# Four bit-operation steps moved in VectorE's queue, and 33 matmuls of nothing in the first three pairs of heads

## The chip, the cores and the metric

The kernel runs on one core of one Trainium2 chip. The metric is the device time of one execution in microseconds (us), the smaller the better. TensorE is PE in the rows, and its weight loads are PEld; VectorE is DVE, ScalarE is ACT, GpSimd is POOL, and SyncE, whose queue issues nearly all DMAs here, is SP.

## The reference, cut to what matters

Three layers follow one another: causal attention with a decay, a gated dense layer, and a layer of eight experts in which each token goes to one.

```python
# attention: q, k, v are (4, 8, 576, 64), f is (4, 8, 576)
scores = q @ k.T / 8 + (cum[:, None] - cum[None, :])   # cum = cumsum(log f)
attn   = softmax(where(causal, -1e9, scores))
x      = attn @ v                                      # -> (2304, 512)
# dense layer
a, b = x @ w1, x @ w2                                  # 512 -> 1024
x    = ((a * b) @ w3) @ w_out                          # the kernel uses Wc = w3 @ w_out
# experts, 8 of them, the one of the largest gate logit
out[mask] = gate * eom * (relu(x[mask] @ w1[e]) @ w2[e])
```

## The kernel before, in words

**Pairs of heads.** Attention works on 16 pairs of heads, n = 0 to 15. Each pair goes through named stages: loads (lk, lq, lv), the rounded high parts of k and q on ScalarE (kh, qh), the scores of the four query blocks and of the last 64 queries on TensorE (X1, X3, X2, X0 and XL, tiles x and xl), their row maxima on VectorE (m1, m3, m2, m0 and mL, line 234), the remainders of k and q on VectorE (kl, ql, line 201), the turn of the maxima (Tm on TensorE, line 241, tc on ScalarE, line 244), their spread by two DMAs into the rows MR (mv, line 174), the transposed scores in four PSUM groups (GA to GD, line 208, from the high parts and the remainders; HA to HD add the decay and the maxima from CK and MR to the same groups), the exponentials (eA to eD, line 270), the causal masks and column sums on GpSimd (a0 to a4, s1 to s3, lines 276 and 288), and the product with v and its sums (p0, p1, p3, su, lines 297 and 313, tile v). ScalarE copies them out (xa, line 317; sa, line 320), SP stores the sums (zs, line 324), and after each fourth pair the sums of a batch are loaded back, inverted on VectorE and stored (rl, rv, rs, lines 333 to 338).

**The order.** Every engine runs its queue strictly in the order of the program. `START` gives each stage a time within its pair, pairs are 9.8 apart (`PERIOD`), and line 378 sorts all stages of all pairs by START + 9.8 n; `AFTER` puts further steps into the last pair's time in the same way. The times only set an order. Those around the change, in the last pair's time, are: mL 3.54, Tm 3.61, tc 3.98, ql 4.35, lv of pair 14 at 5.71, mv 6.59, GA 8.35, HA 8.43, and later xa of pair 14 at 18.04, s1 18.31, rv of pair 11 at 18.4, sa of pair 14 at 18.44, a2 18.51.

**Wc's pieces.** Between the stages the weights w3 and w_out arrive in pieces of 512 KB of 64-bit floats, in the order of line 407 (piece 12 is w_out's j=4, wo4 in the rows; 13 is w04, 14 is w14, 15 is wo5, 16 is w05). `upto(step, n)` (line 460) brings the first n pieces through a step: step 0 is the load on SP (line 439), 1 a copy on ScalarE (446), 2, 3 and 4 are three bit operations on VectorE (448, 450, 452), 5 a rounding on ScalarE, 6 a subtraction on GpSimd. `K4_13` is upto(4, 13), the three bit operations of piece 12; `K0_16` is the load of piece 15. The raw tiles have three buffers, so that the load of piece 15 waits for the last bit operation of piece 12, and the load of piece 16 for that of piece 13. SP issues in order, and what stands behind such a load waits too.

**PSUM.** The scores rotate through three buffers of two banks (`pss`, line 92); the tile v has the remaining two banks, with one buffer (`psv`, line 86). So p0 of a pair writes v only after sa of the pair before has read it. At the start twenty matmuls of a zero tile, 128x512 in bf16, run on TensorE (`warm_up`, line 154).

Of the kernel before, what the change touches and what calls it, by code (L numbers as in the profile page):

```python
# [11 lines left out]
F32 = mybir.dt.float32  # L12
# [3 lines left out]
BF16 = mybir.dt.bfloat16  # L16
# [12 lines left out]
P = 128  # L29
# [29 lines left out]
}  # L59
SHIFT = {}  # L60

AFTER = {
    "K4_13": 3.595, "K0_15": 3.605, "K0_16": 3.615, "K4_14": 3.625, "K0_17": 3.635, "inputs": 11.329, "scores": 13.382,
    "K1_15": 18.064, "K1_16": 18.074, "K4_15": 18.084, "K0_18": 18.094, "K4_16": 18.104, "P0": 28.286, "P1": 28.296,
    "P2": 28.306, "P3": 28.316,
}


# [6 lines left out]
def attention(nc, tc, ident, xT, rz, xs, wc, q, k, v, f):  # L75
# [6 lines left out]
    V, A, G, PE, SP = nc.vector, nc.scalar, nc.gpsimd, nc.tensor, nc.sync  # L82
    with (
# [6 lines left out]
        inputs, scores = ExitStack(), ExitStack()  # L90
# [10 lines left out]
        def decay_parts():  # L101
            SP.dma_start(out=fc, in_=f)
            V.tensor_scalar(out=fc, in0=fc, scalar1=1e-4, scalar2=1.0, op0=ALU.max, op1=ALU.min)
            A.activation(out=fc, in_=fc, func=ACTF.Ln)
            V.tensor_tensor_scan(c8, fc, fc, 0.0, ALU.add, ALU.bypass)
            V.tensor_scalar(out=EK[0:NH], in0=c8, scalar1=-8.0, scalar2=None, op0=ALU.mult)
            V.scalar_tensor_tensor(out=EK[NH:], in0=c8, scalar=-8.0, in1=EK[0:NH].bitcast(F32), op0=ALU.mult, op1=ALU.subtract)
# [15 lines left out]
        def rows(e, t):  # L123
            e.memset(t.bitcast(F32), 0.0)
            for h in range(2):
                e.memset(t[64 * h:64 * h + 3, :min(S, t.shape[1])].bitcast(F32), 1.0)

        def constants():
            rows(G, CKs[0])
            rows(V, OQ)  # L130
            for t in (OD, *QDs, *[t[:, S:] for x in KHs for t in x]):
                V.memset(t.bitcast(F32), 0.0)
            for h in range(2):
                V.memset(OD[64 * h:64 * h + 3, HALF[h]].bitcast(F32), 1.0)
                for t in (OQ, OD):
                    V.memset(t[64 * h:64 * h + 1].bitcast(F32), 0.0)
            V.memset(ones, 1.0)
            for t in Ms:
                V.memset(t, 0.0)
            G.memset(tri, 0.0)  # L140
            G.affine_select(
                out=tri[:, 512:640], in_=tri[:, 512:640], pattern=[[-1, P]],
                compare_op=ALU.is_ge, fill=NEG, base=0, channel_multiplier=1,
            )
            G.memset(tril, 0.0)
            for h in range(2):
                G.affine_select(
                    out=tril[64 * h:64 * h + 64, 512:S], in_=tril[64 * h:64 * h + 64, 512:S],
                    pattern=[[-1, SL]], compare_op=ALU.is_ge, fill=NEG, base=0, channel_multiplier=1,
                )  # L150
            for t in MRs + CKs[1:]:
                rows(G, t)

        def warm_up():

            z = p1.tile([P, 512], BF16, name="warm")
            V.memset(z, 0.0)
            ps = pss.tile([P, 1024], F32, name="warm", tag="s")
            for _ in range(WARM):
                PE.matmul(ps[:, 0:512], z[:, :P], z, start=True, stop=True)  # L160

        st = {}
# [215 lines left out]
        order = [(START[x] + SHIFT.get((n, x), 0.0) + PERIOD * n, n, i, x) for n in range(B * NP) for i, x in enumerate(START)]  # L378
        order = sorted(order + [(t + PERIOD * (B * NP - 1), B * NP, 0, x) for x, t in AFTER.items()])
        with tc.manual_schedule():  # L380
            warm_up()
            decay_parts()
            constants()
            for _, n, _, x in order:
                if x == "inputs":
                    inputs.close()
                    continue
                if x == "scores":
                    scores.close()
                    wc.banks(0)  # L390
                    continue
                if n == B * NP:
                    if x[0] == "K":
                        wc.upto(int(x[1]), int(x[3:]))
                    else:
                        wc.product(*wc.steps.pop(0))
                    continue
                fn, *args = stages[x]
                fn(st[n], *args)


class Combined:
# [801 lines left out]
def program(shapes):  # L1204
    nc = bacc.Bacc("TRN2", target_bir_lowering=False, num_devices=1)
    a = {n: nc.dram_tensor(n, s, mybir.dt.from_np(t), kind="ExternalInput").ap() for n, (s, t) in shapes.items()}
    out = nc.dram_tensor("out", (N, DM), F32, kind="ExternalOutput").ap()
    with tile.TileContext(nc) as tc:
        with tc.tile_pool(name="keep", bufs=1) as keep, tc.tile_pool(name="raws", bufs=2, reuse_waits="tile") as raws, tc.tile_pool(name="div", bufs=1, space=DRAM) as div:
            rz = div.tile([NP, 2, N], F32, name="rz")  # L1210

            xs = div.tile([E * N, DM + 2], F32, name="xs")
            ident = keep.tile([P, P], F32, name="ident")
            make_identity(nc, ident)
            xpool = ExitStack()
            xt = xpool.enter_context(tc.tile_pool(name="xt", bufs=1, side="right"))
            xT = xt.tile([P, NP, N], F32, name="xT")
            region = ExitStack()
            region.enter_context(tc.manual_schedule())
            wc = Combined(nc, tc, xpool, raws, a["wo"], a["w3t"])  # L1220
            attention(nc, tc, ident, xT, rz, xs, wc, a["q"], a["k"], a["v"], a["f"])
            moe(nc, tc, ident, xT, rz, xs, xpool, raws, region, wc, a["w1"], a["w2"], a["gates"], a["e1"], a["e2"], out)
            xpool.close()
    return nc
# [9 lines left out]
```

## Time and profile before

| | |
|---|---|
| median of 3 runs | 854.89 us (850.76 to 856.73) |
| the profiled execution | 857.55 us, span 855.9 us |
| mean granted clock of TensorE | 0.971 of full speed |
| TensorE busy | 800.8 us (94%), 5140 matmuls |
| VectorE, ScalarE, GpSimd busy | 453.7 us, 280.7 us, 373.6 us |

All times in rows are us from the start of the span. The attention part takes about the first 213 us; after it come the products of Wc, the dense layer and the experts. In a row of the order of time, the bracket at the end is the time that the engine stood idle before the row and what ended that. A clock of 1.00 is full speed (2.4 GHz), 0.50 the half (1.2 GHz).

### The profile page before, as it was taken

The numbers are of one execution on the slowest core, as the hardware profiler recorded it, in microseconds if no ns is written. First come the engines' busy times: TensorE is split into PE (matmuls) and PEld (weight loads), VectorE is DVE, ScalarE is ACT, GpSimd is POOL, SyncE is SP. The second block draws the span as 40 slices with busy tenths as digits, with TensorE's granted clock in tenths as the row PEclk, the third lists the DMA queues.
The fourth block names the chain that finished last, engine by engine and source line by source line (L and its number), as shares of the span: only waits on it lengthen the run. The fifth ranks groups of instructions, "written<-read, shape, count | busy, mean of one in ns | idle before, by whom it ended". The sixth has DMA issues, their size and how long they took to land.

```text
span 855.9 us, 13772 instructions
## 1 busy us (share of the span) xinstructions
PE 800.8 (94%) x5140; PEld 654.6 (76%) x5140; DVE 453.7 (53%) x950; ACT 280.7 (33%) x536; POOL 373.6 (44%) x383
## 2 busy tenths in 40 slices
PE   6899989977999899999999999998799999999995
PEld 4666666655887577888788788897588899999983
DVE  7588888872698860341333223135456846346430
ACT  3466655642454422221221221222122222232321
POOL 5578887883574570131013021023245543354521
PEclk7799999996999999999999999999999999999998
DMA  3446666522445211100010010033556654566460
GB/s 113 135 134 198 216 216 211 157 78 84 129 169 171 87 42 35 50 23 28 25 38 19 7 50 1 1 123 124 173 148 221 201 202 138 183 204 209 149 256 28
DMA packets 40340, 102.12 MB, mean 119 GB/s; under 512 B 8610, under 2 KB 9314, under 8 KB 40016
## 3 DMA queue, kind: packets, MB, share of 16 engines
q1 hardware_dynamic: 37088, 91.46, 33.7%
q0 software_dynamic: 3184, 9.77, 3.0%
q8 instruction: 41, 0.67, 0.3%
q14 instruction: 27, 0.22, 0.1%
HBM read 84.47 MB, written 16.51 MB: 118 GB/s over the span
## 4 chain that ended last, share of the span: by engine, by line
PE 63%; DVE 16%; DMA 9%; issue 7%; ACT 2%; SPq 1%; POOL 0%; POOLq 0%; DVEq 0%; ACTq 0%
DVE junk L234 5%; PE y L541 4%; PE y L539 4%; PE y L540 4%; PE h L541 3%; PE h L539 3%; PE h L540 3%; DMA xs<-xr,pos 3%; PE a L539 3%; PE b L539 3%; PE a L541 3%; PE a L540 3%; PE b L540 3%; PE b L541 3%; PE q L539 2%
## 5 line engine op out<-in xcount | busy, mean ns | idle before, releaser
L569 DVE TENSOR_TENSOR ga<-b,ga 128x512 f32<-128x512 f32 (+1 forms) x40 | 25.4, 635 | 149.6 <-PE b L541 146.5
L684 POOL DMA_INDIRECT xs<-xr,pos x18 | 18.9, 1050 | 187.9 <-DVE pos L680 130.6
L234 DVE CUSTOM_DVE_ANT_0 junk<-x,tri 128x256 f32<-128x256 f32 (+3 forms) x128 | 62.7, 489 | 10.4 <-PE x L208 1.3
L539 PE MATMUL h<-gh,ah 128*128 128x320 f32 (+4 forms) x224 | 67.2, 300 | 0.0
L540 PE MATMUL h<-gl,ah 128*128 128x320 f32 (+4 forms) x224 | 66.9, 299 | 0.0
L541 PE MATMUL h<-gh,al 128*128 128x320 f32 (+4 forms) x224 | 66.9, 299 | 0.0
L276 POOL TENSOR_SCALAR_AFFINE_SELECT PT<-PT 128x256 f32<-128x256 f32 (+1 forms) x80 | 42.6, 545 | 48.5 <-ACT PT L270 48.1
L541 PE MATMUL a<-xh,w1l 128*128 128x512 f32 (+1 forms) x160 | 59.8, 374 | 3.0 <-POOL w1l L457 3.0
L539 PE MATMUL a<-xh,w1h 128*128 128x512 f32 (+1 forms) x160 | 60.8, 380 | 1.9 <-ACT w1h L455 1.9
L539 PE MATMUL b<-xh,w2h 128*128 128x512 f32 (+1 forms) x160 | 60.5, 378 | 0.0
L539 PE MATMUL y<-raw,gh 128*128 128x512 f32 x144 | 58.4, 406 | 1.6 <-ACT gh L570 1.6
L540 PE MATMUL b<-xl,w2h 128*128 128x512 f32 (+1 forms) x160 | 60.0, 375 | 0.0
L540 PE MATMUL a<-xl,w1h 128*128 128x512 f32 (+1 forms) x160 | 59.9, 374 | 0.0
L541 PE MATMUL b<-xh,w2l 128*128 128x512 f32 (+1 forms) x160 | 59.3, 371 | 0.0
L541 PE MATMUL y<-raw,gl 128*128 128x512 f32 x144 | 57.4, 398 | 0.9 <-DVE gl L572 0.9
L540 PE MATMUL y<-raw,gh 128*128 128x512 f32 x144 | 57.6, 400 | 0.0
L532 POOL TENSOR_SCALAR bh<-rb 128x1024 fp32r<-128x1024 f32 x28 | 36.0, 1284 | 47.8 <-DMA rb<-e 41.6
L570 ACT ACTIVATE gh<-ga 128x512 fp32r<-128x512 f32 (+1 forms) x40 | 23.6, 589 | 95.8 <-DVE ga L569 95.8
L297 PE MATMUL v<-PT,vr 128*64 128x448 f32 (+4 forms) x384 | 52.4, 412 | 2.2 <-ACT zs L320 2.2
L960 DVE SCALAR_TENSOR_TENSOR hl<-h,hh 128x320 fp32r<-128x320 f32 (+4 forms) x56 | 25.4, 462 | 50.0 <-ACT hh L959 49.1
L288 POOL TENSOR_TENSOR ac<-ac,PT 128x640 f32<-128x640 f32 (+1 forms) x32 | 45.5, 1421 | 1.6
L533 DVE TENSOR_TENSOR bl<-rb,bh 128x1024 fp32r<-128x1024 f32 x28 | 38.5, 1400 | 13.6 <-POOL bh L532 13.6
(610 smaller groups left out, 2216.2 us busy)
## 6 DMA issues: line engine op xcount, KB each, us to landing
ra<-e SPq DMA_DIRECT2D x28, 512.0 KB
rb<-e SPq DMA_DIRECT2D x28, 512.0 KB
w<-w3t SPq DMA_DIRECT2D x16, 512.0 KB
xs<-zero SPq DMA_DIRECT2D x8, 771.0 KB
vr<-v SPq DMA_DIRECT2D x16, 320.0 KB
kr<-k SPq DMA_DIRECT2D x16, 288.0 KB
qr<-q SPq DMA_DIRECT2D x16, 288.0 KB
wo<-wo SPq DMA_DIRECT2D x8, 512.0 KB
```

What stands on the lines that cost most here:

```text
L234: V.tensor_tensor_reduce(out=junk[:, :w], in0=s["x", i][:, 512 * h:512 * h + w] if i < 4 else s["x", i][:, 224:224 + S], in1=tri[:, 640 - ...
L276: G.affine_select(out=t, in_=t, pattern=[[0, 2], [1, w]], compare_op=ALU.is_ge, fill=0.0, base=0, channel_multiplier=-1,)
L288: G.tensor_tensor(out=acc[:, :, q0 - P:], in0=first if j == 1 else acc[:, :, q0 - P:], in1=src, op=ALU.add)
L297: PE.matmul(s["v"][HALF[h], 384 + q0:384 + q1], s["vr"][:, j, HALF[h]], place(s, j, h, q0, q1), start=(j == 0), stop=(j == 4 or q1 == P),)
L532: G.tensor_scalar(out=hi, in0=src, scalar1=1.0, scalar2=1.0, op0=ALU.mult, op1=ALU.mult)
L533: lo_eng.tensor_tensor(out=lo, in0=src, in1=hi.bitcast(F32), op=ALU.subtract)
L539: PE.matmul(ps, ah, bh, start=start and i == 0, stop=False)
L540: PE.matmul(ps, ah, bl, start=False, stop=False)
L541: PE.matmul(ps, al, bh, start=False, stop=stop and i == last)
L569: V.tensor_tensor(out=ga[:, :w], in0=pb[:, :w], in1=ga[:, :w], op=ALU.mult)
L570: A.activation(out=gh[:, f, :w], in_=ga[:, :w], func=ACTF.Copy)
L960: V.scalar_tensor_tensor(out=hl[:, f, :w], in0=ps[:, :w], scalar=0.0, in1=hh[:, f, :w].bitcast(F32), op0=ALU.max, op1=ALU.subtract)
```

## The change: what it does

It changes the order in two places and adds matmuls in six.

First, in the last pair's time `K4_13`, `K0_15`, `K0_16`, `K4_14` and `K0_17` go from 3.595 to 3.635 to 4.4 to 4.44. The six bit operations of pieces 12 and 13 then stand behind ql of pair 15 in VectorE's queue instead of between mL and ql. In SP's queue the three loads keep their place ahead of vr of pair 14 and of MR of pair 15.

Second, `K1_15` to `K4_16` go from 18.064 to 18.104 to 18.5 to 18.54: ScalarE's copies of pieces 14 and 15 behind sa of pair 14, and their bit operations behind rv of pair 11. The end of the input pools ("inputs") goes from ahead of a3 of pair 15 to behind it; the other entries change their numbers but not their order.

Third, after six stages of pairs 0, 1 and 2 a number of matmuls of the zero tile run, 33 in all; they write a tile that takes the buffer of v before its first use. For that the zero tile is made outside `warm_up`.

```diff
+FILL = {(0, "X0"): 5, (0, "XL"): 10, (1, "X0"): 4, (1, "XL"): 4, (2, "X2"): 5, (2, "X0"): 5}
+
 AFTER = {
-    "K4_13": 3.595, "K0_15": 3.605, "K0_16": 3.615, "K4_14": 3.625, "K0_17": 3.635, "inputs": 11.329, "scores": 13.382,
-    "K1_15": 18.064, "K1_16": 18.074, "K4_15": 18.084, "K0_18": 18.094, "K4_16": 18.104, "P0": 28.286, "P1": 28.296,
-    "P2": 28.306, "P3": 28.316,
+    "K4_13": 4.4, "K0_15": 4.41, "K0_16": 4.42, "K4_14": 4.43, "K0_17": 4.44, "inputs": 11.36, "scores": 13.38,
+    "K1_15": 18.5, "K1_16": 18.51, "K4_15": 18.52, "K0_18": 18.53, "K4_16": 18.54, "P0": 28.29, "P1": 28.3, "P2": 28.31,
+    "P3": 28.32,
 }
...
+        z = p1.tile([P, 512], BF16, name="warm")
+
+        def fill(n):
+            if n and "fill" not in st:
+                st["fill"] = psv.tile([P, 1024], F32, name="fill", tag="v")
+            for _ in range(n):
+                PE.matmul(st["fill"][:, 0:512], z[:, :P], z, start=True, stop=True)
+
         def warm_up():
 
-            z = p1.tile([P, 512], BF16, name="warm")
             V.memset(z, 0.0)
...
                 fn, *args = stages[x]
                 fn(st[n], *args)
+                fill(FILL.get((n, x), 0))
```

## Rows read from the trace of the kernel before

**Rows 1.** Windows of TensorE: us, busy (matmuls), granted clock, DMA share, GB/s.
```profile
11.26:24.90 13.64, 9.61 (x64) 0.50 0.45 140
24.90:31.74 6.84, 3.75 (x34) 1.00 0.38 131
31.74:38.52 6.78, 6.63 (x49) 0.50 0.58 182
...
130.72:192.17 61.45, 53.68 (x590) 1.00 0.47 144
...
209.23:212.65 3.42, 3.42 (x21) 0.50 0.46 157
```

**Rows 2.** TensorE in order of time, the six places: start, us, line, tiles, idle before.
```profile
12.45 0.61 PE L226 MATMUL xl<-kh,QD 128*128 128x288 f32 x1 [1.14 <-DVE M L234]
...
15.88 0.69 PE L241 MATMUL xl<-ident,M 128*64 128x128 f32 x2 [2.10 <-DVE M L234]
...
19.89 0.53 PE L208 MATMUL gA<-qh,kh 64*128 64x192 f32 x2 [0.79 <-DVE M L234]
...
27.38 0.43 PE L241 MATMUL xl<-ident,M 128*64 128x128 f32 x2 [0.86 <-DVE M L234]
...
30.32 0.33 PE L208 MATMUL x<-kh,qh 64*128 64x128 f32 x2 [1.25 <-DVE M L234]
...
31.89 0.53 PE L208 MATMUL gA<-qh,kh 64*128 64x192 f32 x2 [1.14 <-DVE M L234]
```

**Rows 3.** Weight loads of the twenty zero matmuls, in order of time.
```profile
3.90 0.15 PEld L160 LDWEIGHTS <-warm 128*128 128x128 bf16 x1 [0.27 <-issue]
4.33 2.53 PEld L160 LDWEIGHTS <-warm 128*128 128x128 bf16 x12 [0.28 <-issue]
```

**Rows 4.** TensorE in order of time: ends of GA to GD at low and full clock.
```profile
25.73 0.40 PE L226 MATMUL xl<-kh,QD 128*128 128x288 f32 x1
...
38.38 0.47 PE L226 MATMUL xl<-kh,QD 128*128 128x288 f32 x1
...
156.57 0.36 PE L208 MATMUL gA<-qh,kh 64*128 64x192 f32 x2 [0.62 <-DVE M L234]
...
160.45 0.40 PE L226 MATMUL xl<-kh,QD 128*128 128x288 f32 x1
...
172.64 0.37 PE L226 MATMUL xl<-kh,QD 128*128 128x288 f32 x1 [1.25 <-DMA QD<-qh]
```

**Rows 5.** VectorE in order of time, around the first moved step.
```profile
185.34 1.86 DVE L448 TENSOR_SCALAR wo4u<-wo4u 128x512 int32<-128x512 int32 x1
...
192.46 0.75 DVE L201 TENSOR_TENSOR ql<-qr,qh 128x576 fp32r<-128x576 f32 x1
```

**Rows 6.** Waits of SP's queue: for what, us in total, times, longest.
```profile
SPq L439 <- DVE wo4u L452: 9.3, 1, 9.3
...
SPq L439 <- DVE w04u L452: 2.2, 1, 2.2
```

**Rows 7.** SP in order of time, the issue of MR.
```profile
193.47 1.15 SPq L174 DMA_DIRECT2D MR<-mt  x2
```

**Rows 8.** TensorE in order of time, the last pair.
```profile
193.27 0.53 PE L208 MATMUL gA<-ql,kh 64*128 64x192 f32 x2 [4.47 <-DVE ql L201]
...
196.93 0.82 PE L208 MATMUL gA<-MR,CK 64*128 64x192 f32 x4 [2.35 <-DMA MR<-mt]
...
202.06 3.07 PE L297 MATMUL v<-PT,vr 128*64 128x128 f32 x24
...
208.05 4.48 PE L297 MATMUL v<-PT,vr 128*64 128x128 f32 x24 [2.20 <-ACT zs L320]
```

**Rows 9.** ScalarE in order of time, around the second moved step.
```profile
206.44 0.65 ACT L446 ACTIVATE w14u<-w 128x512 f32<-128x512 f32 x1
...
207.55 0.40 ACT L320 ACTIVATE zs<-v 128x288 f32<-128x288 f32 x1
```

**Rows 10.** VectorE in order of time, the first inversion after attention.
```profile
218.22 0.61 DVE L335 TENSOR_SCALAR z<-z 128x36 f32<-128x36 f32 x1 [6.47 <-DMA z<-zd]
```

## The prediction

> **What bounds the kernel now.** I read the granted clock first. In the opening of attention TensorE runs at the lower level, 0.50 (1.2 GHz), from 11.26 to 24.90 us, at full level until 31.74, and at 0.50 again until 38.52 [rows 1]; the reader is to see two stretches with 9.61 and 6.63 us of matmuls in them. Then I read TensorE in order of time over the same stretch: six idle times of 0.79 to 2.10 us, all ended by VectorE's maxima [rows 2]. These are the places behind (0, X0), (0, XL), (1, X0), (1, XL), (2, X2) and (2, X0), in that order, where the new matmuls go. The chain of waits runs here through maxima, scores and the groups GA to GD in turn, and each pair hands its end to the next; so what a pair loses early is still there at the end of attention.
>
> At the last pair I read VectorE, SP's queue and TensorE side by side. TensorE waits 4.47 us for ql, and then, after a few matmuls, 2.35 us more for MR [rows 8]. ql runs only at 192.46, behind six bit operations that begin at 185.34 [rows 5]. But MR is issued only at 193.47 [rows 7], since SP stands 9.3 us at the load behind wo4's bit operations and 2.2 us at the one behind w04's [rows 6], and MR's DMAs are behind both. So of the two waits MR's ends last. Further on p0 of pair 15 waits 2.20 us for sa of pair 14 [rows 8], which stands on ScalarE behind two copies of weight pieces [rows 9], and VectorE then stands 6.47 us at the inversion of the last batch [rows 10], which comes out of that same chain by way of two DMAs.
>
> **The matmuls of nothing.** Twelve of their kind load in 2.53 us, 0.21 us each, where the clock is up; ahead of that they stood 0.43 us apart (3.90 to 4.33) [rows 3]. At 0.21 us the six groups take 1.05, 2.11, 0.84, 0.84, 1.05 and 1.05 us against idle times of 1.14, 2.10, 0.79, 0.86, 1.25 and 1.14 [rows 2, 3]: they fit within 0.1 us each. At 0.43 us they take 2.14, 4.28, 1.71, 1.71, 2.14 and 2.14, which is 6.8 us more than the gaps hold. Their cover is VectorE's maxima; without it, at the low clock, that 6.8 is their price.
>
> Opening: in the profiled execution the clock falls at 11.26, when X0 of pair 0 is nearly done, so the first five may run low. XL(0) then starts 1.0 us later, inside the 2.10 us that TensorE waits afterwards, and the ten behind it no longer fit: Tm(0) comes about 1 us late, of which faster scores behind it give back half. I take +0.5 us. The ends are -0.5 (the clock never falls) and +3.2 (1.0 and 2.2, both groups wholly low).
>
> Pair 0: GA to XL(1) takes 25.73 - 19.89 = 5.84 us [rows 2, 4]. The same work at full clock took 160.45 - 156.57 = 3.88 us in pair 12 [rows 4]. If the clock is up: **-1.96 us**; the other end is 0.
>
> Pair 1: 38.38 - 31.89 = 6.49 us against 3.88 [rows 2, 4]: **-2.61 us**; the other end is 0. In both I take the full gain, since with the fills TensorE has no idle time left over 0.3 us there, and in the long stretch from 130.72 to 192.17 the clock stayed at 1.00 [rows 1] across a single idle time of 1.25 us [rows 4].
>
> Sum of the fills: 0.5 - 1.96 - 2.61 = -4.07 us. The tile that they write takes v's buffer before p0(0), behind them on the same engine: nothing.
>
> **Bit operations behind ql.** ql moves to 185.34 and TensorE's 4.47 us for it go. What is late next is MR. The six bit operations now end later by ql's 0.75 us [rows 5], the loads of pieces 15 and 16 go out that much later, and behind them in SP's queue vr of pair 14 and MR of pair 15: **+0.75 us** at the moment that releases HA. The gA matmuls that go early save nothing, since HA stands behind them for MR in any case. Ends: 0, if ql fits into the wait that the first bit operation shows (1.86 us in all), and +1.9, if that wait falls on ql and once more on a bit operation. I take the middle value because ql's own row shows it. GpSimd's queue is not touched.
>
> **Copies behind sa.** sa(14) starts at 206.44 in the place of w14u, not at 207.55 [rows 9]: p0(15) is released 1.11 us earlier. The idle time in front of it falls from 2.20 to 1.1 us, under the 1.25 us over which the clock held [rows 4]. In the trace the clock fell 1.2 us into these matmuls, at 209.23 [rows 1]; the same 24 took 3.07 us for pair 14 and 4.48 for pair 15 [rows 8], so **-1.11 - 1.41 = -2.52 us**. The other end is -1.11, with the clock falling as before. The copies and bit operations of pieces 14 and 15 come 0.4 us later; VectorE's 6.47 us of waiting for z [rows 10] covers them. rv(11) going ahead of bit operations, and the pool's end behind a3, issue nothing new: nothing.
>
> **The sum** is -4.07 + 0.75 - 2.52 = -5.84 us. Against the profiled execution, 857.55 us, that is 851.7. It lay 2.66 us above the median; from the median, 854.89, the sum gives **849.0 us**, which I take.
>
> **Rivals.** (a) One of the three stretches stays low because the clock falls anyway: one of -1.96, -2.61, -1.41 is lost, so about 851.4. For it: the fall at 11.26 lies ahead of the first fill. Against it: the fills leave almost no idle time. 0.20.
>
> (b) The fills do not do what they say: the falls do not come from gaps this short, and the matmuls lie in idle time for nothing. Left are 0.75 - 2.52, that is 853.1. By the Trainium skill, "TensorE: Matmul & The Clock Gate", section "Why this matters for your kernels", a fall follows one idle gap longer than any of these six, which would give this time. The trace speaks against it: the clock fell at 31.74 with no gap above 1.25 us on either side [rows 1, 2]. 0.10.
>
> (c) Slower: the ten matmuls behind XL(0) run low, hold up Tm(0), and every later group meets a low clock too. Then the fills cost 6.8 us, MR 0.75, and the copies save 1.11: +6.5, so 861.3. It decides at Tm(0): if that comes more than 2 us later than 15.88, this is the case. Against it: zeros ran 0.21 us apart in the warm-up once the clock was up [rows 3], so they do raise it. 0.07. A milder form, with a gain in pair 1 only, ends near 854.9: 0.05.
>
> (d) More than forecast: the opening gains 0.5 instead of losing it, and the last pair's groups too run at full clock. From MR's arrival to p0(14) they took 202.06 - 196.93 = 5.13 us [rows 8], low throughout; at the ratio of pair 0 (3.88 of 5.84) that would be 3.4, so -1.7. All of it: -8.5, or 846.4. Against it: with ql early TensorE stands idle for some 7 us ahead of MR instead of 4.47 and 2.35. 0.13.
>
> **How the numbers follow.** The forecast has 0.45, the rivals 0.20, 0.10, 0.12 and 0.13. A measurement of this kernel can tell about 1% from no change, 8.5 us. The forecast is 0.7%, and only (d), with the spread of the runs (850.76 to 856.73), crosses that: faster 0.17, within 0.80, slower 0.03. The range leaves out the slower cases and the far half of (d): 844.5 to 856, about 0.8.
>
> **What would show it.** In the profile after: granted clock near 1.00 from about 16 to 40 us; GA to XL in 3.9 us in pairs 0 and 1; GA of pair 2 about 4 us earlier than before; ql right behind mL(15), and TensorE's only long wait there for MR, which lands somewhat later against mL(15) than the 11.6 us of before (185.34 to 196.93); p0(15) some 0.1 us after sa(14), and about 3 us long. I am wrong if the clock table still shows 0.50 for many us there, if Tm(0) is over 2 us late, or if GA of pair 2 is early and the end of attention is not.

## The result and the profile after

The changed kernel takes **847.88 us** (median of 9 runs, 845.28 to 850.77) against 856.49 of the kernel before (9 runs, 850.76 to 860.11). The ratio is 0.9906 [0.9879, 0.9932]: 8.0 us less, with an interval from 5.8 to 10.4. The profiled execution took 848.34 us, span 846.7, against 857.55 and 855.9; TensorE's mean granted clock is 0.986 where it was 0.971.

First the granted clock of TensorE in the kernel after, to be held against [rows 1] (window in us, its length, busy with its matmuls, granted clock, DMA share, GB/s):

```profile
11.50:39.00 27.50, 26.07 (x211) 1.00 0.48 155
39.00:130.00 91.00, 82.14 (x906) 1.00 0.62 191
130.00:183.00 53.00, 49.77 (x550) 1.00 0.48 150
...
185.00:195.00 10.00, 4.14 (x30) 0.50 0.43 140
195.00:200.00 5.00, 5.00 (x42) 0.74 0.00 0
```

The two stretches of the opening at 0.50 (the lower level, 1.2 GHz) are gone: it is 1.00 (2.4 GHz) from 11.5 until 183. In attention one low stretch is left, in the last pair, behind the wait for MR. Next, TensorE of the kernel after in order of time, the six places of [rows 2] and the ends of [rows 4]:

```profile
11.23 1.25 PE L162 MATMUL fill<-warm 128*128 128x512 bf16 x5
...
13.08 2.33 PE L162 MATMUL fill<-warm 128*128 128x512 bf16 x10
15.88 0.43 PE L250 MATMUL xl<-ident,M 128*64 128x128 f32 x2 [0.47 <-DVE M L243]
...
18.14 1.04 PE L162 MATMUL fill<-warm 128*128 128x512 bf16 x4
19.35 0.35 PE L217 MATMUL gA<-qh,kh 64*128 64x192 f32 x2 [0.17 <-DVE M L243]
...
23.08 0.41 PE L217 MATMUL gD<-qh,kh 64*128 64x320 f32 x2 [0.37 <-ACT PT L279]
...
23.86 0.40 PE L235 MATMUL xl<-kh,QD 128*128 128x288 f32 x1
...
30.20 0.36 PE L217 MATMUL gA<-qh,kh 64*128 64x192 f32 x2
...
34.08 0.40 PE L235 MATMUL xl<-kh,QD 128*128 128x288 f32 x1
```

The fills ran at full clock (5 took 1.25 us and 10 took 2.33, so 0.22 for each further one) and fit: Tm(0) starts at 15.88 as before, and 0.47 us of idle time is left in front of it. GA of pair 2 starts at 40.27 instead of 44.66.

The last pair, on four engines. VectorE of the kernel after, against [rows 5, 10]:

```profile
178.17 0.76 DVE L210 TENSOR_TENSOR ql<-qr,qh 128x576 fp32r<-128x576 f32 x1
...
179.51 2.46 DVE L460 SCALAR_TENSOR_TENSOR wo4u<-wo,wo4u 128x512 int32<-128x512 int32 x1
182.00 0.78 DVE L462 SCALAR_TENSOR_TENSOR wo4u<-wo,wo4u 128x512 int32<-128x512 int32 x1
...
185.88 0.69 DVE L462 SCALAR_TENSOR_TENSOR w04u<-w,w04u 128x512 int32<-128x512 int32 x1
...
209.94 0.74 DVE L344 TENSOR_SCALAR z<-z 128x36 f32<-128x36 f32 x1 [4.19 <-DMA z<-zd]
```

SP's queue of the kernel after, against [rows 7]:

```profile
182.80 0.33 SPq L449 DMA_DIRECT2D wo<-wo  x1
186.60 0.33 SPq L449 DMA_DIRECT2D w<-w3t  x1
...
187.50 1.16 SPq L183 DMA_DIRECT2D MR<-mt  x2
```

TensorE of the kernel after, against [rows 8]:

```profile
190.86 0.82 PE L217 MATMUL gA<-MR,CK 64*128 64x192 f32 x4 [8.71 <-DMA MR<-mt]
...
195.98 3.71 PE L306 MATMUL v<-PT,vr 128*64 128x128 f32 x24
...
201.51 2.92 PE L306 MATMUL v<-PT,vr 128*64 128x128 f32 x24 [1.10 <-ACT zs L329]
```

ql runs right behind the maximum, and the two waits of [rows 8], 4.47 and 2.35 us, have become one of 8.71 us, for MR. MR waits for the same thing as before: SP issues it behind two loads, and each of these for a buffer that the bit operations free. The last one on wo4u ends at 182.78 and the last one on w04u at 186.57; the loads go out at 182.80 and 186.60. On ScalarE of the kernel after zs now precedes the copy, against [rows 9]:

```profile
201.01 0.41 ACT L329 ACTIVATE zs<-v 128x288 f32<-128x288 f32 x1
201.30 0.68 ACT L456 ACTIVATE w14u<-w 128x512 f32<-128x512 f32 x1
```

### The profile page after: what moved, and what is told of

The parts are those of the page before. It is cut to its first block, busy times and chain, and to the rows that moved or that the text cites. A ratio compares the mean times of both kernels' runs of the same rounds, so it can differ in the third digit from the quotient of the medians.

```text
span 846.7 us, 13835 instructions
## 1 busy us (share of the span) xinstructions
PE 799.8 (94%) x5173; PEld 648.9 (77%) x5173; DVE 451.4 (53%) x950; ACT 281.3 (33%) x536; POOL 376.2 (44%) x383
## 4 chain that ended last, share of the span: by engine, by line
PE 60%; DVE 16%; DMA 11%; issue 7%; ACT 3%; SPq 2%; POOL 1%; POOLq 0%; DVEq 0%; ACTq 0%
DVE junk L243 5%; PE y L551 4%; PE y L550 4%; PE y L549 4%; PE h L551 3%; PE h L549 3%; PE h L550 3%; PE a L549 3%; PE b L549 3%; DMA xs<-xr,pos 3%; PE a L551 3%; PE a L550 3%; PE b L550 3%; PE b L551 3%; DMA out<-ot,id 3%
## 5 line engine op out<-in xcount | busy, mean ns | idle before, releaser
L285 POOL TENSOR_SCALAR_AFFINE_SELECT PT<-PT 128x256 f32<-128x256 f32 (+1 forms) x80 | 44.9, 574 | 39.8 <-ACT PT L279 39.6
L306 PE MATMUL v<-PT,vr 128*64 128x448 f32 (+4 forms) x384 | 50.6, 401 | 1.1 <-ACT zs L329 1.1
L543 DVE TENSOR_TENSOR bl<-rb,bh 128x1024 fp32r<-128x1024 f32 x28 | 37.7, 1370 | 15.0 <-POOL bh L542 15.0
```

Of the source, the lines that this page charges most:

```text
L285: G.affine_select(out=t, in_=t, pattern=[[0, 2], [1, w]], compare_op=ALU.is_ge, fill=0.0, base=0, channel_multiplier=-1,)
L306: PE.matmul(s["v"][HALF[h], 384 + q0:384 + q1], s["vr"][:, j, HALF[h]], place(s, j, h, q0, q1), start=(j == 0), stop=(j == 4 or q1 == P),)
L543: lo_eng.tensor_tensor(out=lo, in0=src, in1=hi.bitcast(F32), op=ALU.subtract)
```

## The experiments

Each is timed against the kernel before; the ratio's 95% interval is in brackets.

**The fills alone.** The kernel before with the fills, the order of the last pair as it was.

```diff
+FILL = {(0, "X0"): 5, (0, "XL"): 10, (1, "X0"): 4, (1, "XL"): 4, (2, "X2"): 5, (2, "X0"): 5}
...
+                fill(FILL.get((n, x), 0))
```

> The kernel before with the 33 matmuls of nothing alone; both moved steps are where they were. Theory (three separate effects that add): the clock stays at 1.00 from about 11 to 39 us, XL of pair 2 starts near 34.1 instead of 38.4, the last pair is as before (ql behind the six bit operations, MR landing some 11.6 us behind mL(15)), and the time falls by 4.0 to 5.5 us, ratio 0.9935 to 0.9955. Rival 1 (the fills do nothing and the moves made the gain): ratio 0.999 to 1.001 and low clock in 11 to 25 us as before. Rival 2 (everything comes from the fills): ratio 0.990 to 0.991.

Measured: 0.9919 [0.9886, 0.9952], 847.49 us. That the fills do nothing is out: they bring most of the change's gain. By the central value, -6.9 us, it is more than was expected; the interval holds most of what was expected and all of rival 2. The granted clock is 1.00 from 11.5 to 39 us. XL of pair 2 starts at 33.27, 5.1 us earlier than in [rows 4], and GA of pair 15 at 180.07, 8.3 us earlier than the 188.34 of before; so some 3 us are won between, where there are no fills (taken up below). In the last pair of this kernel TensorE waits for ql and MR, as before:

```profile
185.64 0.53 PE L217 MATMUL gA<-ql,kh 64*128 64x192 f32 x2 [5.10 <-DVE ql L210]
...
188.51 0.82 PE L217 MATMUL gA<-MR,CK 64*128 64x192 f32 x4 [1.57 <-DMA MR<-mt]
```

From GA of pair 15 to the products of Wc it takes 24.45 us here, 23.93 in the changed kernel and 24.91 before. So in these executions the two moves together are worth some 0.5 us beside the fills, and the ratios, 0.9919 and 0.9906, don't tell them from nothing.

**The bit operations alone.** The kernel before with the first move only.

```diff
-    "K4_13": 3.595, "K0_15": 3.605, "K0_16": 3.615, "K4_14": 3.625, "K0_17": 3.635, ...
+    "K4_13": 4.4, "K0_15": 4.41, "K0_16": 4.42, "K4_14": 4.43, "K0_17": 4.44, ...
```

> The kernel before with the first moved step alone: the bit operations of pieces 12 and 13 and the three loads behind ql; no fills, the copies of pieces 14 and 15 where they were. Theory: ql no longer holds TensorE, but MR, behind the loads in SP's queue, lands 0.75 to 1.1 us later, so the time rises by that, ratio 1.001 (0.9995 to 1.002). Rival (ql was the wait that counted): the gA groups start 4.5 us earlier and the time falls by 2 us or more, ratio 0.9975 or less.

Measured: 1.0 [0.9977, 1.0024]. TensorE in its last pair:

```profile
188.03 0.36 PE L208 MATMUL gA<-qh,kh 64*128 64x192 f32 x2
...
197.73 0.82 PE L208 MATMUL gA<-MR,CK 64*128 64x192 f32 x4 [8.71 <-DMA MR<-mt]
```

From GA to HA it takes 9.70 us; before it took 196.93 - 188.34 = 8.59. ql early frees matmuls that then wait for MR, and MR comes 1.1 us later. The interval rules out the rival's 0.9975 only just, and does not tell 1.1 us from nothing; it is the rows that show the step.

**The copies alone.** The kernel before with the second move only.

```diff
-    "K1_15": 18.064, "K1_16": 18.074, "K4_15": 18.084, "K0_18": 18.094, "K4_16": 18.104, ...
+    "K1_15": 18.5, "K1_16": 18.51, "K4_15": 18.52, "K0_18": 18.53, "K4_16": 18.54, ...
```

> The kernel before with the second moved step alone: the copies of pieces 14 and 15 behind sa of pair 14, their bit operations behind rv of pair 11; no fills. Theory: p0 of pair 15 starts 1.1 us earlier, and the time falls by 1.1 us with the clock falling in it as before and by 2.5 us if it stays up, ratio 0.997 to 0.9987. Rival (the tail waits for the weight pieces instead): the later bit operations of piece 14 push the stores, no gain, ratio 1.000 to 1.001.

Measured: 0.9966 [0.994, 0.9992], 2.1 us less by the medians; the rival's 1.000 lies outside the interval. p0 of pair 15 in this kernel, against [rows 8]:

```profile
207.74 2.92 PE L297 MATMUL v<-PT,vr 128*64 128x128 f32 x24 [1.10 <-ACT zs L320]
```

The wait is 1.10 instead of 2.20 us and the matmuls take 2.92 instead of 4.48. Both halves of the step are there.

**Fills of pair 0 only** (15 of the 33), in the changed kernel.

```diff
-FILL = {(0, "X0"): 5, (0, "XL"): 10, (1, "X0"): 4, (1, "XL"): 4, (2, "X2"): 5, (2, "X0"): 5}
+FILL = {(0, "X0"): 5, (0, "XL"): 10}
```

> The changed kernel with the fifteen matmuls of nothing of pair 0 alone. Theory (each stretch needs its own): the clock stays up through GA to GD of pair 0, falls again near 31 to 32 us, and GA to GD of pair 1 run low; XL of pair 2 starts at 36 to 37 us instead of 33.2 to 34.1, ratio to the kernel before 0.993 to 0.996. Rival (once up, the clock stays): XL of pair 2 below 35 us, ratio 0.990 to 0.991.

Measured: 0.9964 [0.994, 0.9989]. Its granted clock:

```profile
11.50:28.00 16.50, 12.48 (x106) 1.00 0.51 165
28.00:30.00 2.00, 0.86 (x10) 0.85 0.45 124
30.00:36.00 6.00, 6.00 (x47) 0.50 0.50 154
```

The clock holds through the two places that are filled, and through a first gap of 1.14 us that is not (ahead of GA of pair 0, at 19.34). It falls behind the next three, where TensorE stands 0.86, 1.23 and 1.14 us. So one gap of such a length did not bring a fall here, and several in a row did. XL of pair 2 starts at 35.87, just ahead of the expected 36 to 37, and not below 35 as the rival has it.

**Fills of pairs 1 and 2 only** (18 of the 33).

```diff
+FILL = {(1, "X0"): 4, (1, "XL"): 4, (2, "X2"): 5, (2, "X0"): 5}
```

> The changed kernel with the eighteen matmuls of nothing of pairs 1 and 2 alone. Theory: the clock falls near 11 us as before, GA to GD of pair 0 run low for most of their length, XL of pair 1 starts near 25.7 us as before, and pair 1 runs at full clock; ratio to the kernel before 0.993 to 0.995, and this loss and that of the run with pair 0 alone add up to what the fills bring together. Rival (pair 1's stretch alone holds the gain): ratio 0.990 to 0.992.

Measured: 0.9938 [0.9913, 0.9964]. Its granted clock:

```profile
13.50:20.00 6.50, 3.79 (x20) 0.50 0.39 132
20.00:40.00 20.00, 19.80 (x194) 1.00 0.50 159
```

The ratio came as expected. The place in the trace did not: the clock was back at 20, not near 25 [rows 1], so XL of pair 1 came at 24.03 and not at 25.7. What was expected overlooked where the first of these fills lies: X0 of pair 1 runs ahead of GA of pair 0, and so do the four matmuls behind it. The first of them run low, and GA of pair 0 then starts 0.59 us later than before, but at full clock:

```profile
19.44 1.12 PE L162 MATMUL fill<-warm 128*128 128x512 bf16 x3 [0.34 <-issue]
```

In the profiles of three kernels without any fill (before, the bit operations alone, the copies alone) XL of pair 1 came at 25.70 to 26.38.

**Half the fills** (17).

```diff
+FILL = {(0, "X0"): 3, (0, "XL"): 5, (1, "X0"): 2, (1, "XL"): 2, (2, "X2"): 3, (2, "X0"): 2}
```

> The changed kernel with about half the matmuls of nothing in each place, 17 instead of 33 (3, 5, 2, 2, 3, 2). It leaves 0.4 to 1.1 us idle in each place, as the later pairs have at full clock (0.6 us ahead of GA). Theory: that is enough, the clock stays at 1.00 from 11 to 39 us, ratio to the kernel before 0.990 to 0.992. Rival (the places must be filled): a stretch at 0.50 comes back, ratio 0.993 or more.

Measured: 0.9925 [0.9897, 0.9954], which the interval tells neither from the changed kernel nor from the rival's 0.993. Its granted clock:

```profile
12.00:14.00 2.00, 2.00 (x8) 0.50 0.24 90
...
16.00:40.00 24.00, 21.31 (x213) 1.00 0.54 171
```

And TensorE of it in order of time:

```profile
15.88 0.43 PE L250 MATMUL xl<-ident,M 128*64 128x128 f32 x2 [0.61 <-DVE M L243]
```

In this execution the clock did fall in the opening, against what was expected, and it cost nothing: Tm(0) still starts at 15.88, because the fewer fills fit at the low clock too. From 16 to 40 us the clock stayed up, across gaps of 0.41 to 0.60 us.

**Twice the fills** (66).

```diff
+FILL = {(0, "X0"): 10, (0, "XL"): 20, (1, "X0"): 8, (1, "XL"): 8, (2, "X2"): 10, (2, "X0"): 10}
```

> The changed kernel with every number of matmuls of nothing doubled, 66 instead of 33. Theory (they cost nothing only because they fit into the idle time; the clock was up already): 33 more at 0.21 us are 7.0 us, the idle time left in the six places is about 1.4 us, so the time rises by 5 to 7 us against the changed kernel, ratio to the kernel before 0.997 to 1.000. Rival (the time there is set by VectorE, and TensorE's part is hidden anyway): a rise under 2 us, ratio 0.993 or less.

Measured: 0.9987 [0.9967, 1.0007]. TensorE of this kernel:

```profile
14.15 4.26 PE L162 MATMUL fill<-warm 128*128 128x512 bf16 x19
18.35 0.43 PE L250 MATMUL xl<-ident,M 128*64 128x128 f32 x2
```

The clock is 1.00 from 11 to 40 us, and still the gain is gone: Tm(0) comes 2.5 us late, and GA of pair 2 starts at 44.70, as before. A fill is free only as far as the gap holds it.

**A fill in the wait for MR.** The changed kernel, and 40 more matmuls of the zero tile that add zero to GA's sums of pair 15, ahead of HA.

```diff
+                if (n, x) == (15, "GA"):
+                    for _ in range(40):
+                        PE.matmul(st[n]["g", "A"][:, 0:480], z[:, :P], z[:, 0:480], start=False, stop=False)
```

> The changed kernel with 40 more matmuls of zeros behind GA of pair 15, added to GA's own bank, in the 8.7 us in which TensorE waits for MR. Theory (the low clock from about 183 to 197 us comes from that idle time): GA to GD behind MR and p0 of pair 14 run at full clock, 2 to 3 us less, ratio to the kernel before 0.987 to 0.989. Rival (the stretch behind is limited by the exponentials or the masks): under 1 us less, ratio 0.990 or more.

Measured: 0.9877 [0.984, 0.9913]. TensorE of this kernel:

```profile
181.03 8.27 PE L412 MATMUL gA<-warm 128*128 128x480 bf16 x40
190.06 0.51 PE L217 MATMUL gA<-MR,CK 64*128 64x192 f32 x4 [0.76 <-DMA MR<-mt]
...
192.88 2.92 PE L306 MATMUL v<-PT,vr 128*64 128x128 f32 x24
```

From HA to p0(14) it takes 192.88 - 190.06 = 2.82 us instead of 195.98 - 190.86 = 5.12, and p0(14) itself 2.92 instead of 3.71. The wait is as long, but the clock behind it is full. The interval reaches the rival's 0.990; the rows decide against it, since from HA to the products of Wc it takes 11.13 us instead of 14.23.

**MR ahead of the loads.** The changed kernel with the two loads behind MR in SP's queue.

```diff
-    "K4_13": 4.4, "K0_15": 4.41, "K0_16": 4.42, "K4_14": 4.43, "K0_17": 4.44, ...
+    "K4_13": 4.4, "K0_15": 4.41, "K4_14": 4.43, "K0_16": 6.6, "K0_17": 6.61, ...
```

> The changed kernel with one more edit: the loads of pieces 15 and 16 go behind MR of pair 15 in SP's queue (6.6 and 6.61 instead of 4.42 and 4.44). Theory (the last pair's end is set by MR standing behind those two loads): MR is issued within 1 us of its copy at about 179 us instead of 187.5, HA starts at about 182.5 instead of 190.9, and the time falls by 5 to 8 us against the changed kernel, ratio to the kernel before 0.981 to 0.985. Rival (another wait, the masks on GpSimd or the weight pieces, ends only a little sooner): less than 2 us against the changed kernel, ratio 0.988 or more.

Measured: 0.9829 [0.9795, 0.9864]. TensorE of this kernel:

```profile
183.40 0.41 PE L217 MATMUL gA<-MR,CK 64*128 64x192 f32 x4
...
193.25 4.62 PE L306 MATMUL v<-PT,vr 128*64 128x128 f32 x24 [3.50 <-DMA vr<-v]
```

The 8.71 us are gone whole, and the matmuls from HA to p0(14) run at full clock. The next one late is vr of pair 15, which is still behind a load; behind that wait the clock is low again, and p0(15) takes 4.62 us instead of 2.92.

**The old order of the bit operations, once MR is early.** The kernel above with the six back between mL and ql.

```diff
-    "K4_13": 4.4, "K0_15": 4.41, "K4_14": 4.43, "K0_16": 6.6, "K0_17": 6.61, ...
+    "K4_13": 3.595, "K0_15": 3.605, "K4_14": 3.625, "K0_16": 6.6, "K0_17": 6.61, ...
```

> The kernel with MR ahead of the two weight loads, but the six bit operations back between mL and ql, as in the kernel before. Theory (ql is the wait that ends last only once MR is early): TensorE waits for ql until some 7 us behind mL, HA starts 4 to 5 us later than with the bit operations behind ql, ratio to the kernel before 0.987 to 0.989. Rival (the bit operations' place is worth nothing in either order): ratio 0.982 to 0.985.

Measured: 0.9863 [0.9838, 0.9888], a little under what was expected. TensorE of this kernel:

```profile
185.50 0.53 PE L217 MATMUL gA<-ql,kh 64*128 64x192 f32 x2 [5.10 <-DVE ql L210]
```

Now ql's wait is the last; HA follows it at 186.60 without one. The difference to the kernel above is 0.0034 of the time, some 2.9 us: what the first move is worth where MR no longer covers it. The two intervals overlap, so the size is rough, but the rows agree: from GA of pair 15 to the products of Wc it takes 18.93 us here and 15.95 in the kernel above.

**vr ahead as well.** MR and vr of pair 15 both ahead of the loads.

```diff
-SHIFT = {}
+SHIFT = {(15, "lv"): -8.91}
...
-    "K4_13": 4.4, "K0_15": 4.41, "K0_16": 4.42, "K4_14": 4.43, "K0_17": 4.44, ...
+    "K4_13": 4.4, "K0_15": 4.41, "K4_14": 4.43, "K0_16": 6.61, "K0_17": 6.62, ...
```

> The kernel with MR ahead of the two weight loads, and the load of v of pair 15 put ahead of them too. Theory (behind MR the next wait is that load, issued at 189.3 behind the piece of w3): p0 of pair 15 starts near 190.9 instead of 193.3 and stays at full clock, and the stores behind it come 2.5 to 4 us sooner, ratio to the kernel before 0.978 to 0.981. Rival (the stores wait for the weight piece 14 and the sums for GpSimd anyway): under 1 us, ratio 0.982 or more.

Measured: **0.9804 [0.9775, 0.9832]**, 838.55 us, about 1% under the changed kernel. TensorE of this kernel:

```profile
189.67 2.92 PE L306 MATMUL v<-PT,vr 128*64 128x128 f32 x24 [1.10 <-POOL ac L297]
```

p0(15) now starts 3.6 us ahead of the 193.25 of the kernel with MR alone, and 18.4 ahead of the 208.05 of [rows 8], and it runs at full clock. The interval overlaps that of the kernel with MR alone and reaches the rival's 0.982, so the size of this last step is rough. GpSimd's additions are now the largest part, 37.7%, of the chain of waits from 178 to 206 us.

**The zero stores later.** The kernel above with "cr", the stage that stores zeros to memory, at 8.9 instead of 7.59. QD is the copy of the last 64 queries that XL reads; two small DMAs make it.

> The kernel with MR and v of pair 15 ahead of the weight loads, and the zero stores (771 KB each, pairs 4 to 11) behind the small QD copies in SP's queue instead of ahead of them. Theory (XL of pair 10 waits 2.5 to 4 us for QD because QD stands behind that store): the wait falls under 1.5 us, ratio to the kernel before 0.977 to 0.979. Rival (QD waits behind the loads of the weight piece and of rz just as long): ratio 0.980 or more.

Measured: 0.981 [0.9775, 0.9846], no gain over the kernel above, so neither the theory's ratio nor the rival's reason came. Its waits of TensorE from 60 to 180 us (for what, us in total, times, longest):

```profile
PE x L217 <- ACT qh L203: 3.1, 2, 2.2
...
PE xl L235 <- DMA QD<-qh: 0.2, 1, 0.2
```

The wait for QD went from 3.4 to 0.2 us, as it was meant to, and a wait for qh took its place.

## Why the prediction was right, point by point

The forecast of 849.0 us was 1.1 us from the median. That is closer than the sum deserves, by luck: it was reckoned from 854.89, the median of three runs, where nine runs gave 856.49, and the gain was larger than the sum, 8.0 us (5.8 to 10.4) against 5.84. The mechanism came as forecast in the opening and in the last pair; what the sum left out lies between them. Compared at marks in the two profiled executions, after less before (the last column is what was won or lost since the mark above):

| mark | forecast so far | measured so far | what the step made |
|---|---|---|---|
| GA of pair 0 | +0.5 | -0.54 | -0.54 |
| GA of pair 2 | -4.07 | -4.39 | -3.85 |
| GA of pair 15 | -4.07 | -7.18 | -2.79 |
| HA of pair 15 | -3.32 | -6.07 | +1.11 |
| products of Wc | -5.84 | -8.16 | -2.09 |

**Opening: mis-sized.** The +0.5 supposed that the first fills run low. They ran at full clock, and the end -0.5 of the bounds came. The half kernel shows that the fall can come all the same, and that it is free if the fills still fit.

**Pairs 0 and 1: right.** Pair 1 took 34.08 - 30.20 = 3.88 us, the figure taken from pair 12. Pair 0 took 4.51, so 1.33 us were won there instead of 1.96: gD started 0.74 us behind gC's last matmul, where in pair 1 it was 0.20, and 0.37 of it TensorE stood for ScalarE's exponential. In the kernel with the fills alone pair 0 took 23.23 - 19.35 = 3.88 too, and from GA of pair 0 to GA of pair 2 it won 4.66 us, against the forecast's 4.57. Rival (b), by which fills are for nothing, is out: alone they give 0.9919, and the changed kernel with the fills of pair 0 only, or of pairs 1 and 2 only, has 0.9964 or 0.9938 instead of 0.9906. These two losses, 0.0058 and 0.0032, add up to 0.0090, which the intervals don't tell from the 0.0081 of the fills alone. The rule of the Trainium skill, "TensorE: Matmul & The Clock Gate", section "Why this matters for your kernels", asks against drops that long idle gaps be avoided; here the clock also fell behind gaps of 0.86 to 1.25 us in a row and held where they were filled, so the measurement decides against resting on that alone.

**Rival (a)** did not come: no stretch of the opening stayed low, and p0(15) ran in 2.92 us. (By its own terms its time is 850.4 to 851.6, 851.0 in the mean, and not 851.4.) **Rival (c)** did not come either, but the doubled kernel shows half of its mechanism, at full clock: Tm(0) 2.5 us late takes back the whole gain.

**Not in the sum: pairs 2 to 15.** The prediction let the gain of the opening pass unchanged to the end of attention. It grew by 2.79 us. In the seven profiles with these 33 fills (the changed kernel, the fills alone and five with more edits) it grew by 0.62 to 3.21, so the sign holds and the size is one execution's.

Of the 2.79, 0.68 lie between GA of pair 9 and GA of pair 10 (14.09 us before, 13.41 after). XL(10) waits there for QD. Before, and after:

```profile
127.74 0.58 PE L226 MATMUL xl<-kh,QD 128*128 128x288 f32 x1 [2.60 <-DMA QD<-qh]
...
123.97 0.37 PE L235 MATMUL xl<-kh,QD 128*128 128x288 f32 x1 [3.30 <-DMA QD<-qh]
```

The wait is 0.7 us longer after, but the granted clock behind it is 1.00, where before it is 0.50 from 127.74 to 130.72. This is a low stretch that the prediction passed over. The profiles divide by it: the stretch takes 13.06 to 13.41 us in the five in which the clock holds behind that wait, and 14.09 to 16.82 in the nine in which it falls there (in the kernel with the zero stores later, behind the wait for qh). The length of the wait does not tell which: the clock held behind 3.30 us and fell behind 2.50, in the kernel with pair 0's fills.

Another 1.83 lie between GA of pairs 13 and 14 (12.50 to 10.67). Ahead of XL(14) it is 1.05: the wait for QD there is 1.25 us before [rows 4] and 0.19 after. Behind XL(14) it is 0.78, where ql of pair 14 meets an addition of GpSimd's. Before (VectorE and GpSimd in order of time):

```profile
174.45 2.43 POOL L288 TENSOR_TENSOR ac<-PT 128x896 f32<-128x896 f32 x1
...
174.83 2.67 DVE L201 TENSOR_TENSOR ql<-qr,qh 128x576 fp32r<-128x576 f32 x1
```

and after:

```profile
168.94 0.84 DVE L210 TENSOR_TENSOR ql<-qr,qh 128x576 fp32r<-128x576 f32 x1
...
170.49 2.10 POOL L297 TENSOR_TENSOR ac<-PT 128x896 f32<-128x896 f32 x1
```

Where GpSimd's addition starts first, ql takes 2.67 us; where ql is done first, 0.84. The profiles divide by this: ql(14) took 2.66 or 2.67 us in four of them (before, the copies alone, the fills of pair 0, the fills of pairs 1 and 2), with 12.5 to 13.1 us between GA of pairs 13 and 14, and 0.84 or 0.95 in the others, with 10.4 to 11.0. In the four XL(14) had waited 1.25 to 1.76 us for QD, in the others at most 0.93 for anything. So a late QD, which brings XL(14) and all behind it later, comes together with a ql behind the addition; that the one brings the other is read from the order of the rows, and no run changed it alone. The bit operations alone, without any fill, are among the short ones (11.0), and two kernels with fills are among the long ones. So the fills by themselves do not decide it; but all nine profiles with fills in all six places are short, and with one profile of each kernel it stays open how much of this comes with the fills and how much is chance. In such marks, therefore, one profile cannot tell a step of 2 us from an order that turned over.

**Bit operations: right, somewhat dearer.** MR became the last wait and came later: +1.11 instead of +0.75, and +1.1 in the kernel with that move alone. ql's 0.76 us is the larger part; the rest is in the bit operations, where one took 2.46 us.

**Copies: right.** The release came 1.10 us earlier and the matmuls of p0(15) were 1.56 faster (forecast 1.11 and 1.41). The step made -2.09 instead of -2.52, as p0(14) took 3.71 us instead of 3.07, its clock coming up later. That is not shown to be the copies' doing: with the copies alone p0(14) took 3.71 as well, but 2.92 with half and with twice the fills, where they stand likewise.

**Rival (d)** was half right: its opening came, its full clock in the last pair did not, against which the prediction had put the longer stand ahead of MR. The fill in that wait shows what lay there: 2.3 us from HA to p0(14), where 1.7 was reckoned.

The span is 9.2 us shorter, and the inversion of the last batch [rows 10] comes 8.28 earlier; the 0.9 behind it, in the parts after attention, was not pursued.

## What to carry to other kernels

A gap that another engine's short step leaves on TensorE can cost more behind it than its own length: look at the granted clock after it, and fill it with work of nothing, but only with as much as it holds, at the low clock too. When one of two waits in a row is removed, read which ends last, and follow that one through the queue that issues it: here the first move gained nothing until MR stood ahead of the loads that wait for buffers, and then vr was the next one late. A small DMA in an in-order queue is as late as the latest thing ahead of it. And before a step is put down to the change, look whether it also turns up between kernels that don't differ in it.

## What the runs showed of the hardware that was not expected

The half kernel's 17 zero matmuls held the clock at 1.00 from 16 to 40 us as the 33 did. Forty of them in a wait of nearly 9 us kept the clock full behind it. Unfilled, the clock fell behind a wait of 2.60 us (before) and held behind one of 3.30 (after).

VectorE's subtraction for ql, with two operands in SBUF, takes 0.84 us or 2.67 us by whether GpSimd's addition started ahead of it. The Trainium skill, "SBUF — State Buffer", section "SBUF: two separate sides", has the two share a port pair that the first one holds for its whole instruction. The traces agree: in the long form ql ends 0.62 us behind the end of the addition (177.50 against 176.88), near the 0.76 that ql of pair 15 takes by itself.
